# One order for all operations of an attention + gMLP kernel, from an offline search, with the eight PSUM banks given out per use

## The chip, the cores and the metric

The kernel runs on one core of one Trainium2 chip. The metric is device time in microseconds (us) of that core, the median of several executions. Before the change it was 281.91 us (three runs, 281.49 to 283.92). All medians below are of fast runs alone.

The runs of this study were made on several chips of the same kind, and the chips do not give the same time for the same program: the kernel before takes 282 to 283 us on some (283 on chip 11 of the record) and 316 to 321 us on others (chips 0 and 15). Kernels are therefore compared only with runs of the kernel before on the same chip in the same call. Where I set two chips beside each other, the text says so.

## The reference

Four batches, eight heads, 768 tokens, head dimension 64, and block-sparse attention in blocks of 32: each query block sees its neighbours, the first and the last block (the "global" ones) and three sampled blocks. The first and the last query block see all keys. A gated MLP with spatial mixing follows.

```python
mask = np.abs(blk_i - blk_j) <= 1
mask = mask | (blk_i == 0) | (blk_j == 0) | (blk_i == 23) | (blk_j == 23)
for qb in range(24):
    for kb in sampled_blocks[qb]:
        mask[qb*32:(qb+1)*32, kb*32:(kb+1)*32] = True
attn = softmax(np.where(mask, q @ k.T / sqrt(64), -1e9)) ; x = (attn @ v) as [B, 768, 512]
h = gelu(x @ w_in)                    # 512 -> 1024
u, v = h[..., :512], h[..., 512:]
v_n = layer_norm(v) * g_ln
v_s = einsum('ts,bsd->btd', w_sg, v_n) + b_sg[None, :, None]
out = x + (u * v_s) @ w_out
```

## The kernel before

The program is a list of about 1,200 named operations. Each names its engine, what it reads and writes, an estimated duration and a priority. The names recur below: `qkW qkG qkR qkQ` are score matmuls (window, global, random, and the two full query blocks), `ex*` the exponentials on ACT, `pvG pvW pvR pvQ` the products with v, `rec nrm` the normalization on DVE; `TRk TRq` transpose keys and queries and `ek eq` evict them; `xT xE` transpose and evict the attention output; `mV mU gV gU` are the first MLP matmul and its gelu, `mS g1 g2` spatial mixing and gate, `mO res` the output matmul and the residual. `ga` gathers v blocks from a scratch tensor in DRAM, `sc` writes that tensor, `vg va vs` read regular parts of it, and `kp kr` copy sampled key blocks in SBUF. A number after the name is the batch, then the tile of 128 tokens (`pvR3.0`).

A greedy list scheduler orders the operations while the kernel is built, and takes PSUM from three fixed pools:

```python
    Sps = ctx.enter_context(nc.psum_tensor("Sps", [P, 2048], F32))   # scores: two pairs of banks
    Ops = ctx.enter_context(nc.psum_tensor("Ops", [P, 1024], F32))   # PV output: one pair
    Mps = ctx.enter_context(nc.psum_tensor("Mps", [P, 1024], F32))   # all else: two banks
    pl.pool("S", 2); pl.pool("O", 1); pl.pool("M", 2)
    ...
    def schedule(self):
        ...
            for e in engs:
                cands = []
                for o in ready[e]:
                    t, s = avail(o)          # when inputs and a PSUM place are there
                    ...
                    cands.append((max(t, free[e]) + ..., o.prio, o.idx, o, s, pen))
                tmin = min(c[0] for c in cands)
                c = min((c for c in cands if c[0] <= tmin + 0.03), key=lambda c: (c[1], c[2]))
```

`emit` turns the dependences into semaphore waits and writes out, for each engine, its own list in order. Two more things matter. SyncE reads 21 block numbers into registers in one operation, ahead of the v scratch write; and some starts are held back by hand (`aft`), such as the v load of batch 1 behind the gather of block 12:

```python
    def regs_sp(e):
        for j in range(3):
            load_regs(e, "SP", j, SPSET)                              # seven blocks
        return e.dma_start(scr[1][768:800, :], scr[0][768:800, :])
    op("SP", "regsS", regs_sp, r=["IDX", ("scz", 0)], w=["regS", ("scz", 1)], ...)
    ...
    if b == 0 and i == HOLD1: hold[1] = [o]                           # ldv1 waits for this gather
```

The gate uses one buffer `gt`; `xE` of every batch runs on ACT. All matmuls but the transposes go through one helper, so their line is always L326 (L303 after): read such groups by their tiles.

The softmax here doesn't subtract the row's maximum and nothing guards it: scores larger than these inputs give would overflow.

## Time and profile before

```profile
span 314.7 us, 8868 instructions
PE 234.8 (75%) x3717; PEld 171.5 (55%) x3717; DVE 163.7 (52%) x468; ACT 149.1 (47%) x222; POOL 104.8 (33%) x204
PE   1543047597737479787699999787799997999994
PEclk9999999969795758779799999899599999999999
```

By stretches (busy time with instruction counts for the five engines, then granted clock, DMA share, GB/s):

```profile
0.00:40.00 40.00, 13.44 (x277) 10.35 (x277) 15.67 (x79) 19.19 (x26) 13.24 (x39) 1.00 0.78 252
40.00:160.00 120.00, 83.19 (x1533) 63.77 (x1532) 48.95 (x140) 55.40 (x80) 55.20 (x92) 0.82 0.72 156
160.00:300.00 140.00, 128.78 (x1871) 92.05 (x1871) 90.27 (x236) 74.52 (x116) 36.40 (x75) 0.95 0.31 78
```

TensorE is idle 27 of the first 40 us, 37 of the next 120 and 11 of the next 140. Note the span: 314.7 us, where the timed median is 281.91.

```profile
PE Sps L326 <- ACT PW L721: 4.1, 4, 2.9
PE Mps L504 <- ACT QT L512: 3.2, 4, 0.9
PE Sps L326 <- ACT PW L668: 3.0, 2, 2.7
PE Ops L326 <- issue: 2.1, 2, 1.3
```
A wait of PV for the normalization of the one output pair is in the table too, further down: 0.6 us.

```profile
80.77 0.82 ACT QT L512
...
81.63 0.54 PE Mps L504 x12
...
82.20 0.82 ACT QT L512
```

```profile
39.70 0.61 PE L326 MATMUL Sps<-QT,KR 64*128 64x32 bf16 x32 [10.32 <-POOL KR L600]
40.24 0.62 PE L326 MATMUL Ops<-VG,PG 128*128 128x130 bf16 x4
```

### The profile page before, as it was taken

Reading aid. Unit: us, or ns where it says so; the run is one execution under the profiler, and the core shown is the slowest. Engines: PE = TensorE matmul, PEld = TensorE weight load, DVE = VectorE, ACT = ScalarE, POOL = GpSimd, SP = SyncE. Lnnn points to the kernel's source line nnn. Section 1 sums busy time; section 2 is a strip of 40 time slices with the busy share of each in tenths; the row PEclk is TensorE's granted clock in tenths of the full one; section 3 lists DMA queues with packets and bytes.
Section 4 is the critical chain, followed back from the end, with each engine's and each line's share of the span. In section 5 each row is a group of like instructions: output and inputs, shape, how many; then the busy total and the mean of one; then the engine's idle time right before and its main releaser. Section 6 shows DMA issues by size and latency. Waiting matters only on the chain.

```text
span 314.7 us, 8868 instructions
## 1 busy us (share of the span) xinstructions
PE 234.8 (75%) x3717; PEld 171.5 (55%) x3717; DVE 163.7 (52%) x468; ACT 149.1 (47%) x222; POOL 104.8 (33%) x204
## 2 busy tenths in 40 slices
PE   1543047597737479787699999787799997999994
PEld 1432036485626357565355868565567675767642
DVE  6525013236533165425498657354477665758683
ACT  2587024356334752636212587455425874755200
POOL 1131777112183851542441222653403124102100
PEclk9999999969795758779799999899599999999999
DMA  6957863980999929331799102442711014111022
GB/s 205 374 164 288 230 162 78 173 133 40 195 275 242 308 33 214 86 92 38 206 210 261 64 6 50 133 122 60 211 68 32 4 27 120 37 69 35 0 100 100
DMA packets 34411, 41.29 MB, mean 131 GB/s; under 512 B 6548, under 2 KB 27700, under 8 KB 34372
## 3 DMA queue, kind: packets, MB, share of 16 engines
q0 software_dynamic: 14112, 17.40, 27.9%
q1 hardware_dynamic: 20260, 23.33, 24.0%
q8 instruction: 29, 0.48, 0.6%
q14 instruction: 10, 0.08, 0.1%
HBM read 39.45 MB, written 9.55 MB: 156 GB/s over the span
## 4 chain that ended last, share of the span: by engine, by line
PE 58%; DVE 14%; issue 11%; ACT 9%; POOL 3%; another core or an unknown queue 2%; DVEq 1%; POOLq 0%; ACTq 0%
PE Mps L326 28%; PE Ops L326 12%; PE Sps L326 9%; PE Mps L795 5%; PE Mps L504 4%; DVE gt L856 3%; ACT PR L700 2%; DVE xg L859 2%; DVE KT L512 2%; ACT QT L512 2%; POOL VR L579 1%; PE Mps L620 1%; DVE x_tok L780 1%; DVE x_tok L874 1%
## 5 line engine op out<-in xcount | busy, mean ns | idle before, releaser
L579 POOL DMA_INDIRECT VR<-scr,IDX x60 | 56.2, 937 | 56.7 <-PE Ops L326 29.7
L596 DVE COPY KR<-KT 128x128 bf16 x176 | 27.4, 230 | 38.7 <-PE Ops L326 20.8
L326 PE MATMUL Mps<-w_sgT,vh 128*128 128x384 bf16 x192 | 38.0, 345 | 2.7 <-DVE KT L512 1.8
L700 ACT ACTIVATE PR<-Sps 96x1024 bf16<-96x1024 f32 x20 | 20.4, 1020 | 32.9 <-PE Ops L326 21.6
L600 POOL COPY KR<-KT 128x128 bf16 x88 | 22.5, 296 | 39.1 <-PE Sps L326 27.1
L326 PE MATMUL Mps<-w_out,xg 128*128 128x512 f32 x96 | 28.6, 429 | 2.8 <-DVE xg L859 1.6
L326 PE MATMUL Mps<-xg,w_in 128*128 128x384 f32 x128 | 28.3, 375 | 2.5 <-ACT QT L512 2.0
L856 DVE SCALAR_TENSOR_TENSOR gt<-Mps,gcol,bsg 128x384 f32<-128x384 f32 x32 | 19.8, 618 | 17.8 <-PE Mps L326 15.6
L326 PE MATMUL Mps<-w_in,xg 128*128 128x512 f32 x96 | 27.6, 434 | 1.5 <-ACT xg L798 0.7
L326 PE MATMUL Sps<-QT,KR 64*128 64x32 bf16 x704 | 13.6, 178 | 19.2 <-POOL KR L600 9.7
L798 ACT ACTIVATE xg<-Mps 128x512 fp32r<-128x512 f32 x24 | 14.3, 596 | 28.3 <-PE Mps L795 21.0
L326 PEld LDWEIGHTS Mps<-xg,w_in 128*128 128x128 f32 x128 | 23.3, 205 | 6.9 <-ACT QT L512 2.3
L326 PEld LDWEIGHTS Mps<-w_sgT,vh 128*128 128x128 bf16 x192 | 17.6, 101 | 16.9 <-DVE KT L512 2.2
L814 ACT ACTIVATE vg<-Mps 128x512 f32<-128x512 f32 x24 | 14.0, 598 | 26.8 <-PE Mps L326 25.2
L326 PE MATMUL Sps<-QT,KT 64*128 64x64 bf16 x544 | 16.9, 209 | 12.7 <-issue 3.8
L821 POOL TENSOR_TENSOR lnt<-lnmv,lnc 128x2 f32<-128x2 f32 x12 | 3.0, 248 | 69.7 <-DVE lnmv L817 69.7
L512 DVE COPY KT<-Mps 128x768 bf16<-128x768 bf16 x16 | 15.1, 954 | 20.3 <-PE Mps L504 17.2
L326 PE MATMUL Ops<-VA,PW 128*64 128x65 bf16 x384 | 21.7, 206 | 3.9 <-issue 3.7
L326 PEld LDWEIGHTS Sps<-QT,KR 64*128 64x128 bf16 x704 | 10.9, 96 | 23.3 <-POOL KR L600 9.8
L326 PEld LDWEIGHTS Mps<-w_in,xg 128*128 128x128 f32 x96 | 18.0, 204 | 8.6 <-DVE x_tok L874 2.0
L326 PEld LDWEIGHTS Mps<-w_out,xg 128*128 128x128 f32 x96 | 16.9, 193 | 9.6 <-DVE xg L859 2.5
L326 PEld LDWEIGHTS Sps<-QT,KT 64*128 64x128 bf16 x544 | 12.1, 105 | 17.9 <-issue 5.5
(91 smaller groups left out, 414.0 us busy)
## 6 DMA issues: line engine op xcount, KB each, us to landing
out_dram<-x_tok SPq DMA_DIRECT2D x20, 256.0 KB, 2.1
scr<-vj SPq DMA_DIRECT2D x4, 780.0 KB, 5.0
VR<-scr SPq DMA_DIRECT2D x84, 32.5 KB, 3.3
VS<-scr SPq DMA_DIRECT2D x4, 650.0 KB
vn<-in_v_dram POOLq DMA_DIRECT2D x3, 768.0 KB, 9.1
kn<-in_k_dram POOLq DMA_DIRECT2D x3, 768.0 KB
qn<-in_q_dram POOLq DMA_DIRECT2D x3, 768.0 KB, 13.9
VA<-scr SPq DMA_DIRECT2D x4, 520.0 KB
```

Of the source, the lines that this page charges most:

```text
L326: return pe.matmul(o, l, r, start=start, stop=True, skip_group_check=True)
L504: ins = pe.transpose(Mbf[64 * hp:64 * hp + 64, c:c + P], n_[:, 2 * pp + hp, j, :], ident[:, :])
L512: return x.activation(o_, i_, ACT.Copy) if nm == "q" else x.tensor_copy(o_, i_)
L579: return g.indirect_dma_start(out=VR[0:96, rg, :, :].rearrange("p h e -> p (h e)"), out_offset=None, in_=scr[bp][:, :], in_offset=bass.Ind ...
L596: ins = x.tensor_copy(KR[:, :, rg, 32 * j:32 * j + 32], KT[:, :, bass.ds(vals["DVE", j, i], 32)])
L600: op("POOL", f"kp{b}.{i}", lambda x, i=i, rg=rg: x.tensor_copy(KR[:, :, rg, 64:96], KT[:, :, bass.ds(vals["POOL", 2, i], 32)]), r=kk + [(" ...
L700: return a.activation(PR[pr_][0:96, :], Sps[0:96, uR.slot * 1024:uR.slot * 1024 + 1024], ACT.Exp, scale=SCALE)
L795: ins = pe.transpose(Mps[:, cc:cc + P], x_tok[bp][:, tau, kt * P:kt * P + P], ident_f[:, :])
L798: op("ACT", f"xE{b}.{tau}", lambda a: a.activation(xg[c][:, :, tc * P:tc * P + P], Mps[:, u.slot * 512:u.slot * 512 + 512].rearrange("p (a ...
L814: op("ACT", f"gV{b}.{tau}", lambda a: a.activation(vg[vr][:, :], Mps[:, u.slot * 512:u.slot * 512 + 512], ACT.Gelu_apprx_tanh), r=[("vp", ...
L856: op("DVE", f"g1{b}.{c}{dt}", lambda x: x.scalar_tensor_tensor(gt[gr][:, :], Mps[:, u.slot * 512:u.slot * 512 + 384], gcol[:, dt:dt + 1], ...
L859: op("DVE", f"g2{b}.{c}{dt}", lambda x: x.tensor_tensor(xg[2 + c][:, dt, :], gt[gr][:, :], uT[c][:, dt, :], ALU.mult), r=[("gt", gr), ("uT ...
```

## The change

The intent: replace the greedy order by one found by a long offline search over a model of the schedule, and free the search from the PSUM pools. The whole order, with a bank for each use of PSUM, is now a string of 1,228 operations; the kernel only checks it and turns it into waits. No arithmetic is removed.

```diff
-SEMLAT = 0.07
+XE = ("DVE", "ACT", "ACT", "ACT")
...
-    def schedule(self):
-        ...                                    # the list scheduler, and the pools
+    def arrange(self, seq, bank):
+        ...
+        held = [None] * 8
+        for o in seq:
+            assert all(d.pos < o.pos for d in o.deps), o.name
+            u = o.alloc
+            if u is None: continue
+            u.slot = bank[o.name]
+            for i in range(u.banks):
+                h = held[u.slot + i]
+                if h is not None:
+                    o.deps = o.deps + [x for x in h.readers if x not in o.deps]
+                held[u.slot + i] = u
+        self.order = {e: [o for o in seq if o.eng == e] for e in ("PE", "ACT", "DVE", "POOL", "SP")}
...
+SEQ = """
+krz bias0 ones lnc zero ident0 ident1 ldq0.3 sbi ldk0.0 csq0.3 TRq0.3:3 ldv0.0 csv0.0 bias1 ix0 ldk0.1 ...
+ldq0.1 regsD1 csq0.1 TRq0.1:0 ldv1 regsP0 regsP1 regsS15 ldq0.0 csq0.0 eq0.1 regsS3 regsP2 regsS6 sc0 ...
+...                                            # 1,228 operations; ":3" is the (first) PSUM bank
...
-    gt = [sb(f"gt{i}", [P, 384], F32) for i in range(1)]
+    gt = [sb(f"gt{i}", [P, 384], F32) for i in range(2)]
-    Sps, Ops, Mps and their pools
+    PS = ctx.enter_context(nc.psum_tensor("PS", [P, 4096], F32))
-    def regs_sp(e): ...                        # 21 register loads and a DMA in one operation
+    for i in SPSET:                            # seven operations, and the DMA apart
+        op("SP", f"regsS{i}", rs_, r=["IDX"], w=[("regS", i)], ...)
-        op("ACT", f"xE{b}.{tau}", ...)
+        op(XE[b], f"xE{b}.{tau}", ...)
```

Scores and PV outputs take two neighbouring banks, all else one. The holds `aft` are ignored, so the v load of batch 1 (`ldv1`) is issued as early as its place on POOL allows.

## The prediction

> **What bounds the kernel now.** By the busy table TensorE works 234.8 of 314.7 us (75%); DVE 52%, ACT 47%, POOL 33%. By stretches TensorE is busy 13.4 of the first 40 us, 83.2 of 120 us in 40-160 (69%), 128.8 of 140 us in 160-300 (92%), 9.4 of the last 15. So the start is bound by transfers, batches 0/1 by waits, batches 2/3 nearly TensorE-bound, a tail paced by DVE. In the chain of waits TensorE has 58%, DVE 14%, issue 11%. The profiled span is 33 us over the timed median of 281.91, with a granted clock of 0.59 to 0.82 over 60-140 us. Batches 2 and 3 repeat with a 63.5 us period, so I put most of these 33 us in batches 0/1 and don't count them as gain.
>
> **What changes.** No arithmetic goes. Instruction counts and bytes stay; ACT table loads stay at about ten (1.28 us each). Six 0.6 us evictions move from ACT to VectorE.
>
> 1. Start. SyncE reads 21 registers from 13.7 to 23.7 us, and only then issues the v scratch write (24.4; landed about 30.1); TensorE idles 9.7 us until 38.6, since key copies stand behind six gathers on POOL. The change puts three of the seven register groups ahead of that write, loads v earlier, and puts key copies before gathers. I expect the write at about 20, landing at 26. Against that: batch 1's v load now has no wait ahead of it on POOL, so it issues at about 2 us, when the DMA share is already 0.96 to 1.07 (6-15 us). [...] Net: first PV matmul at 35-38 instead of 39.1; gain 2-4 us.
> 2. Batches 0/1. One output pair and two M banks become any of eight, so PV need not wait for the 0.21+0.69 us normalization, and key/query transposes (idle 0.9 us between, 88-97 us) overlap their evictions. Timed gain estimated 6-8 us.
> 3. Batches 2/3: idle is 8%, some 11 us in 140; two gt buffers and finer interleaving recover about half: 5 us.
> 4. Tail: g1/g2 pairs alternate with TensorE through one gt (0.63+0.57 us, eight times; 295-308 us). Gain 2-3 us.
>
> **On the critical path:** about 17 us of 282. [...]
>
> **Prediction:** 265 us (6% faster), 8 in 10 between 252 and 277. Faster by over 2%: 0.84; within 2%: 0.12; slower: 0.04.
>
> **What would show it.** Busy times per engine within 3% except DVE +4, ACT -4 us (clock aside); TensorE idle in 40-160 down from 37 us to under 25; idle in the batch-2/3 stretch under 7 us; scratch write issued before 22 us; first PV matmul by 38; batch-1 v load issued at about 2 us, first score matmul after 22; tail (first batch-3 gate matmul to end) near 18 instead of 21 us.
>
> **What would make it wrong.** A fixed order can't adapt: if real DMA landings or POOL times differ from the model, one late gather stalls every engine behind it and the gain of batches 0/1 goes. If the timed run already has little idle there, only start and tail count: 275. [...]

The sum came to about 17 us: 2 to 4 at the start, 6 to 8 in batches 0/1, 5 in batches 2/3, 2 to 3 in the tail.

## More of the kernel before

Below, a "fast chip" is one on which the kernel before takes 282 to 283 us, a "slow chip" one on which it takes 316 to 321.

The prediction had one profile of this kernel. Its lines, first of the page: span, busy time of each engine (share of span, instructions), TensorE's busy tenths in 40 slices of the span, and the clock that TensorE was granted, in tenths.

```profile
0.00:45.50 45.50, 15.90 (x373) 12.28 (x373) 17.67 (x90) 22.07 (x31) 16.06 (x45) 1.00 0.80 242
45.50:170.30 124.80, 101.94 (x1730) 77.25 (x1730) 68.85 (x186) 67.52 (x101) 56.76 (x95) 0.90 0.80 170
170.30:246.70 76.40, 72.70 (x1480) 54.16 (x1478) 52.93 (x151) 50.12 (x76) 28.01 (x58) 0.98 0.31 87
246.70:281.70 35.00, 29.12 (x136) 18.92 (x136) 22.71 (x43) 9.29 (x16) 2.68 (x6) 1.00 0.20 68
```

(The clock of 1.00 in the first row is not borne out by the durations of the matmuls there; the fourth call takes this up.) In the stage of batches 0 and 1 (second row) TensorE is still idle 22.9 of 124.8 us and gets 0.90 of its clock; in the next stage it is idle 3.7 of 76.4.

At the start, from the timelines of SyncE's queue and of TensorE: the scratch write is issued at 23.08 us, the reads of the global v rows at 31.29, and TensorE waits 10.32 us for key copies before its first PV matmul at 40.24.

```profile
23.08 0.56 SPq L531 DMA_DIRECT2D scr<-vj  x1
...
31.29 2.55 SPq L541 DMA_DIRECT2D VG<-scr  x4
```

The chain of waits shows the first two lines at work (start, length, what). The first piece: ACT loads a table, then runs an exponential, and only then the score matmuls get the place in `Sps` that it frees. The second: a query transpose fills one of the two `Mps` banks and must wait for an eviction each time.

```profile
69.13 1.28 ACT L721
...
70.42 1.03 ACT PW L721
...
71.50 0.61 PE Sps L326 x16
```

The run that was profiled took 316.53 us itself. So the profile is no distorted copy of the timed runs but an honest record of a slower run. The prediction had to guess where the 33 us lay.

That can be settled by a control made later: the same kernel, unchanged, profiled on a chip where it takes 283 us (experiment c0_before). All comparisons with the kernel after use this profile. (It is of another call than the result's, but of the same speed: the kernel before takes 283.12 us there and 282.3 in the result.) Its page lines, and its stretches, cut at landmarks of the work (first normalized tile of batch 0, first of batch 2, last of batch 3):

```profile
span 281.7 us, 8868 instructions
PE 219.7 (78%) x3717; PEld 162.6 (58%) x3717; DVE 162.2 (58%) x468; ACT 149.0 (53%) x222; POOL 103.5 (37%) x204
PEclk9999999999795759997999999999799999999999
```

## The result, and the profile after

| | before | after |
|---|---|---|
| time, median of 4 fast runs each | 282.3 us (281.49 to 283.92) | 250.3 us (249.55 to 251.99) |
| ratio, 95% interval | | 0.887 (0.880 to 0.893) |
| span of the profile used here | 281.7 us | 247.7 us |
| mean granted clock in it | 0.952 | 0.977 |

Ratios are the mean time of one kernel's fast runs over that of the other's of the same rounds, so not quite the ratio of the medians quoted. Executions over 1.5% slower than the fastest of the same kernel are left out of the means. The change brought 32 us where 17 were predicted, and 250.3 lies just below the range that should have held it (252 to 277).

The page and the stretches of the kernel after, cut at the same landmarks:

```profile
span 247.7 us, 8892 instructions
PE 205.8 (83%) x3717; PEld 158.6 (64%) x3717; DVE 159.9 (65%) x474; ACT 142.3 (57%) x216; POOL 110.2 (44%) x204
PEclk9999999989999979999999997999999999999999
```

```profile
0.00:40.60 40.60, 14.14 (x300) 11.25 (x301) 18.00 (x79) 18.66 (x26) 18.93 (x47) 1.00 1.01 276
40.60:147.30 106.70, 97.52 (x1899) 75.82 (x1897) 73.91 (x215) 69.15 (x104) 57.43 (x96) 0.97 0.89 190
147.30:216.20 68.90, 67.35 (x1380) 50.87 (x1378) 45.91 (x140) 46.05 (x70) 31.14 (x55) 0.98 0.37 103
216.20:247.70 31.50, 26.80 (x145) 20.64 (x143) 22.05 (x44) 8.45 (x17) 2.67 (x6) 0.98 0.23 84
```

Side by side, in us (lengths from the two tables of stretches; idle is length less TensorE busy):

| stage | before | after | gain | predicted gain | TensorE idle before, after |
|---|---|---|---|---|---|
| start, to first tile of batch 0 | 45.5 | 40.6 | 4.9 | 2 to 4 | 29.6, 26.5 |
| batches 0/1, to first tile of batch 2 | 124.8 | 106.7 | **18.1** | **6 to 8** | 22.9, 9.2 |
| batches 2/3, to last tile of batch 3 | 76.4 | 68.9 | 7.5 | 5 | 3.7, 1.6 |
| tail | 35.0 | 31.5 | 3.5 | 2 to 3 | 5.9, 4.7 |
| sum | 281.7 | 247.7 | 34.0 | 17 | 62.0, 41.9 |

Three of the four terms came out within some 2.5 us of what was said; one is more than twice too small. Inside it, the first normalized tile of batch 1 comes at 111.2 us before and at 91.3 after: 15.0 of the 18.1 us lie between the first tiles of batches 0 and 1. The stages do not hold quite the same work, since the new order moves matmuls between them (counts in brackets: 1730 in batches 0/1 before, 1899 after, 100 fewer in batches 2/3), so the split into stages is good to a few us only. That is also why batches 2/3 could gain 7.5 us with only 3.7 us of idle time: part of their work is now done earlier.

Of the 34.0 us, TensorE's idle time gave 20.1 and its busy time 13.9 (219.7 to 205.8), with the same 3717 matmuls. Weighing the busy time of each 1-us window of the two profiles with what its recorded clock lacks of full speed, I estimate 11.5 us lost to the clock before and 4.9 after: 6.6 of the 13.9. (The sum leaves out the start, where the recorded clock fails; TensorE is busy there for 15.9 and 14.1 us, so little of the difference can hide in it.) So busy time was no fixed quantity of work here: it shrank by 6% without any work taken away. The other 7.3 us I have not taken apart.

The waits of the batch-0/1 stage after the change answer to the four lines shown of before:

```profile
PE PS L303 <- issue: 6.4, 4, 3.4
PE PS L303 <- DVE QT L493: 0.9, 1, 0.9
PE PS L303 <- DMA VG<-scr: 0.6, 1, 0.6
```

No wait for an exponential to free a score place, none for an eviction to free a transpose bank is left among them. What remains is mostly "issue", time for which the profile shows no cause. Its largest piece, 3.39 us at 45 us, lies inside one group of 32 score matmuls, after the third of them; `emit` puts a group's semaphore waits before its first matmul only.

At the start (queue of SyncE, then TensorE):

```profile
19.60 0.36 SPq L510 DMA_DIRECT2D scr<-vj  x1
...
28.60 1.40 SPq L520 DMA_DIRECT2D VG<-scr  x2
```

```profile
26.56 1.03 PE L303 MATMUL PS<-QT,KT 64*128 64x64 bf16 x32 [2.80 <-DVE QT L493]
...
37.81 0.62 PE L303 MATMUL PS<-VG,PG 128*128 128x130 bf16 x4 [5.54 <-DMA VG<-scr]
```

The scratch write is issued 3.5 us earlier, the first PV matmul comes 2.4 us earlier, and in exchange the first score matmul slipped from 19.79 (timeline of c0_before) to 26.56, as predicted (after 22).

### The profile page after: what moved, and what is told of

Same layout as the page of the kernel before. It is cut to its first block, busy times and chain, and to the rows that moved or that the text cites. A ratio compares the mean times of both kernels' runs of the same rounds, so it can differ in the third digit from the quotient of the medians.

```text
span 247.7 us, 8892 instructions
## 1 busy us (share of the span) xinstructions
PE 205.8 (83%) x3717; PEld 158.6 (64%) x3717; DVE 159.9 (65%) x474; ACT 142.3 (57%) x216; POOL 110.2 (44%) x204
## 4 chain that ended last, share of the span: by engine, by line
PE 67%; DMA 17%; issue 5%; SPq 4%; POOL 2%; DVE 2%; ACT 1%
PE PS L303 58%; DMA uT<-in_v_dram 5%; PE PS L774 5%; DMA x_tok<-in_moe_w_sg_dram 5%; PE PS L483 4%; DMA VG<-scr 3%; DMA VR<-scr,IDX 3%; SPq L445 1%; POOL VR L558 1%; ACT vj L460 1%; SPq L520 1%; SPq L390 1%; DMA scr<-VG 1%; POOL KR L579 1%; PE PS L599 1%
## 5 line engine op out<-in xcount | busy, mean ns | idle before, releaser
L303 PE MATMUL PS<-w_sgT,vh 128*128 128x384 bf16 x192 | 35.2, 332 | 0.0
L679 ACT ACTIVATE PR<-PS 96x1024 bf16<-96x1024 f32 x20 | 20.3, 1021 | 12.4 <-PE PS L303 12.4
L303 PE MATMUL PS<-xg,w_in 128*128 128x384 f32 x128 | 27.4, 348 | 0.0
L303 PE MATMUL PS<-w_in,xg 128*128 128x512 f32 x96 | 26.9, 408 | 0.0
L303 PE MATMUL PS<-w_out,xg 128*128 128x512 f32 x96 | 26.8, 409 | 0.0
L838 DVE SCALAR_TENSOR_TENSOR gt<-PS,gcol,bsg 128x384 f32<-128x384 f32 x32 | 19.6, 616 | 9.5 <-PE PS L303 8.9
L303 PEld LDWEIGHTS PS<-w_sgT,vh 128*128 128x128 bf16 x192 | 17.6, 99 | 11.5 <-issue 0.7
L303 PEld LDWEIGHTS PS<-xg,w_in 128*128 128x128 f32 x128 | 22.2, 188 | 2.0 <-ACT xg L780 0.4
L796 ACT ACTIVATE vg<-PS 128x512 f32<-128x512 f32 x24 | 14.1, 601 | 11.5 <-PE PS L303 11.0
L659 ACT ACTIVATE PG<-PS 128x512 bf16<-128x512 f32 x24 | 14.0, 600 | 10.1 <-PE PS L303 10.1
L303 PEld LDWEIGHTS PS<-QT,KT 64*128 64x128 bf16 x544 | 11.5, 104 | 12.9 <-issue 5.0
L303 PEld LDWEIGHTS PS<-w_out,xg 128*128 128x128 f32 x96 | 17.0, 188 | 3.4 <-DVE xg L841 0.2
L303 PE MATMUL PS<-VA,PW 128*64 128x65 bf16 x384 | 18.4, 203 | 0.0
```

Of the source, the lines that this page charges most:

```text
L303: return pe.matmul(o, l, r, start=start, stop=True, skip_group_check=True)
L659: op("ACT", f"exG{b}.{tau}", aft=ga, fn=lambda a: a.activation(PG[pg_][:, :], PS[:, uG.slot * 512:uG.slot * 512 + 512], ACT.Exp, scale=SCALE),
L679: return a.activation(PR[pr_][0:96, :], PS[0:96, uR.slot * 512:uR.slot * 512 + 1024], ACT.Exp, scale=SCALE)
L796: op("ACT", f"gV{b}.{tau}", lambda a: a.activation(vg[vr][:, :], PS[:, u.slot * 512:u.slot * 512 + 512], ACT.Gelu_apprx_tanh), r=[("vp", b ...
L838: op("DVE", f"g1{b}.{c}{dt}", lambda x: x.scalar_tensor_tensor(gt[gr][:, :], PS[:, u.slot * 512:u.slot * 512 + 384], gcol[:, dt:dt + 1], b ...
```

## The experiments

Theory A: with the same engines at the same speed, the old order left about 23 us of idle time in batches 0/1 even on a fast chip; the new order and its banks fill most of it, and some of the clock dips go with it. I had taken that idle time for a fault of the first profile. Rival B: the eight banks alone do it, in any order. Rival C: the start is what counts, and shifts everything behind it. Rival D: it is the clock.

### First call: what the first profile was worth, and order against banks (before: 283.12 us)

**c0_before**: the kernel before, unchanged.

> The kernel before, unchanged, as a control with a clean profile. Expected 282 us (281 to 284). The first profile of it spanned 314.7 us at a granted clock of 0.91, 33 us over the timed runs. Theory A (the 33 us are a clock and trace matter of that one execution): this profile spans about 280 at a clock above 0.95, and TensorE idles 25 to 30 us less between 40 us and the end of batch 1. Rival B (timed runs are like the first profile in their idle share): the profile again spans over 300.

Measured: 283.18 us, ratio 1.0005 (0.996 to 1.005), span 281.7. TensorE idle 24.0 of 100 us between 40 and 140. Span and clock are as Theory A had them; the idle time is not: from 40 us to the last tile of batch 1 it falls from 34.6 to 22.4 us, 12 us less and not 25 to 30. The lines are shown above. By landmarks, the first profile's surplus of 33 us lay as follows: 2.6 us before the first tile of batch 0 (48.1 against 45.5), 19.0 in batches 0/1 (143.8 against 124.8), 11.5 in batches 2/3 (87.9 against 76.4), none in the tail. So "most" of it was in batches 0/1, as the prediction had it, but taking it away still leaves 22.9 us of idle time there, and of the 23.2 us that the first profile lost to the clock, 11.5 are lost on the fast chip as well.

**b_banks8**: the old order, eight banks given out by least recent use, one `gt`, `xE` on ACT. It tests rival B by itself.

```diff
-    pl.schedule()
+    SEQ = the order that schedule() gives for the kernel before, written out
+    bank  = the least recently used of eight, for each use of PSUM
-XE = ("DVE", "ACT", "ACT", "ACT")
+XE = ("ACT", "ACT", "ACT", "ACT")
```

> The order of before on all engines, but each PSUM use takes the least recently used of eight banks; one gt buffer, all xT evictions on ACT as before. Order theory: 277 to 283 us. Bank theory: 268 us or less.

Measured: 273.86 us, ratio 0.971 (0.964 to 0.978). Free banks in the old order are worth 3%, a quarter of the gain. Between the two theories. Of its profile, the stage of batches 0 and 1:

```profile
45.20:164.40 119.20, 99.47 (x1729) 76.78 (x1730) 70.23 (x187) 67.17 (x101) 55.82 (x94) 0.90 0.83 177
```

This stage takes 124.8 us in c0_before, on the same chip, and 119.2 here: 5.6 us by the banks alone.

**b_greedy8**: the old scheduler run again, with eight banks to choose from instead of pools.

```diff
-                pl = self.pools[o.alloc.pool]
-                for s in range(len(pl["held"])):
+                for s in (range(8) if n == 1 else (0, 2, 4, 6)):
+                    us = [held8[s + i] for i in range(n)]
+                    ...                        # with at most four banks for scores, four for outputs
```

> The old list scheduler run again with eight banks (scores and single-bank uses at most four each, outputs at most four), so the old rule makes a new order with the new freedom. Order theory (the search itself matters): 270 to 280 us. Bank theory (any scheduler with eight banks gets it): 262 us or less.

Measured: 269.04 us, ratio 0.951 (0.945 to 0.956), just better than the range of the order theory. A greedy order made for eight banks is worth 5%. The remaining 6 points belong to the searched order with its own banks; the second `gt` buffer, which this variant lacks, is in them too. The stage of batches 0 and 1 takes 113.3 us, 11.5 less than in c0_before:

```profile
44.90:158.20 113.30, 93.96 (x1776) 75.05 (x1772) 66.87 (x187) 64.68 (x100) 58.27 (x96) 0.89 0.89 187
```

**a_psum_old**: the new order on the old pools. Where a use found no free place in its pool, the operation had to move back: 75 of 343 TensorE operations change place, by at most 7; on the other engines 162 of 885, by at most 10.

```diff
-TRk0.0:1 ... TRk0.1:6 ... qkW0.0:4 ... pvG0.0:6
+TRk0.0:6 ... TRk0.1:7 ... qkW0.0:0 ... pvG0.0:4     # scores 0-1 or 2-3, output 4-5, all else 6 or 7
```

> The new order, but PSUM given out as before (two score pairs, one output pair, two single banks); operations are only put back as far as a missing bank demands (75 of 343 TensorE steps change place, by 7 places at most). Order theory (the gain is the order on the engines): 252 to 258 us, most of the 32 us stays. Bank theory (the gain is that PSUM may be given to any use): 268 us or more, over half of the gain goes.

Measured: 347.09 us in its one fast run, slower than any theory allowed: 23% over the kernel before. The other three (356.21 to 359.77) count as slow, since they lie over 1.5% above it, so there is no interval. The profile is of one of the slow three (mean clock 0.837, against 0.876 in the fast run), so it shows what kind of waits there are and not how much each costs the fast run. Its clock row, and what TensorE waits for after 45 us:

```profile
PEclk9999999786799967658579998995555999558999
```

```profile
PE PS L304 <- ACT QT L492: 7.4, 9, 0.9
PE PS L304 <- DVE x_tok L760: 6.4, 6, 2.0
PE PS L304 <- ACT uT L824: 5.2, 9, 0.6
```

TensorE waits for the readers of PSUM: for the evictions of query transposes, for the normalization of the one output pair (`x_tok`), for the gelus of MLP outputs. So the searched order is not a better order in itself; it is one that needs free banks. (An order searched for the old pools was not tried, and the repair here is a simple one.) Order and banks are not two gains that add: banks without the order give 3%, the order without the banks costs 23%, both give 11%.

### Second call: where in the run (another chip; before: 321.05 us)

**hyb_a_then_b**: the new order up to the first normalized tile of batch 1 (431 operations), then the old one, with eight banks. **hyb_b_then_a**: the reverse (456 operations). They tell a local gain from a shift that everything later inherits. In the first, the banks before the seam are the searched ones and 172 of the 200 after it were chosen anew; in the second, 247 of all 283 were.

```diff
-SEQ = new
+SEQ = new[:431] + [o for o in old if o not in new[:431]]       # hyb_a_then_b
+SEQ = old[:456] + [o for o in new if o not in old[:456]]       # hyb_b_then_a
```

> The new order up to the first normalized tile of batch 1 (431 operations), then all the rest in the order of before, with eight banks. By the landmarks of the two profiles this tile comes at 111.2 us before and 91.3 us after, so stage-local theory: 282 less about 20, 258 to 266 us. Rival (the gain needs the whole order, because the new order hands less work on at the seam): 270 us or more.

> The order of before up to the first normalized tile of batch 1 (456 operations), then the rest in the new order, eight banks. Stage-local theory: 282 less about 14, 264 to 272 us, plus what eight banks alone give the first part (0 to 5 us less). Rival: 275 us or more.

Measured: 286.5 us, ratio 0.893 (0.886 to 0.901), and 294.9, ratio 0.920 (0.910 to 0.930). The expectations had been written for a fast chip, so compare ratios. The gains are 10.7% and 8.0%. They sum to 18.7%, and the whole change is worth 18.8% on a chip of this speed (c1_after, next call), but that agreement is in part luck: both variants hold some of what eight banks give to the old order, and neither has the searched banks throughout. The landmarks say more. The times until the first normalized tile of batch 1, and from there to the end (us; all at the slow chips' speed, though not all on one chip):

| | to this tile | rest |
|---|---|---|
| kernel before (first profile) | 124.9 | 189.8 |
| hyb_a_then_b | 93.0 | 193.5 |
| hyb_b_then_a | 120.0 | 173.1 |
| kernel after (c1_after) | 92.9 | 166.6 |

With the new order first, the early gain is all there and the rest is about as long as before (3.7 us longer). With the new order last, the rest gains 16.7 us although the start is the old one; 4.9 of the gain lie before the seam, where only the banks are new. So the gain is made where the order differs and is not handed on. For the whole change the tile comes 32.0 us earlier and the rest gains 23.2, so 58% is made before it; the profiles of the fast chips say the same (4.9 + 15.0 of 34.0 us, 59%). Rival C in its strong form is out.

**a_lru8**: the new order, but the banks chosen anew by a rule close to least recent use; 248 of 283 choices differ.

```diff
-TRq0.3:3 ... TRk0.0:1 ... qkW0.0:4 ...     # banks from the search
+TRq0.3:b ... TRk0.0:b ... qkW0.0:b ...     # b chosen anew; 248 of 283 differ
```

> The new order unchanged on every engine, but the bank of 248 of the 283 PSUM uses chosen anew (roughly least recently used). If only order and freedom count: 250 to 253 us. Rival (the search tuned the banks to the order, so that a bank is free when its use comes up): 257 us or more.

Measured: 280.32 us, ratio 0.875 (0.865 to 0.884). At first sight this is the ratio of the change itself, 0.887. That was wrong: the 0.887 is from a chip where the kernel before takes 282 us, this one from a chip where it takes 321. The next call corrects it.

**b_start**: the kernel before, with three of SyncE's seven register groups and the DMA that stood with them moved behind the scratch write and its reads.

```diff
 SyncE:
-regsS3 regsS6 regsS9 regsS12 regsS15 regsS18 regsS21 scz1 sc0 vg0 va0 vs0
+regsS3 regsS6 regsS9 regsS12 sc0 vg0 va0 vs0 regsS15 regsS18 regsS21 scz1
```

> The kernel before with its own order and PSUM pools; on SyncE alone three of seven register groups and one small copy move behind the v scratch write and reads. I expect the scratch write to issue at 20 to 21 us instead of 24.4 and the whole to take 2 to 4 us less: 278 to 281 us. If start transfers are limited by the DMA engines and not by that issue: no change, 282 to 284 us.

Measured: 315.6 us, ratio 0.981 (0.971 to 0.992). The scratch write went out at 19.77 us (24.43 in the first profile, which is the one of a slow chip to compare with). So the point that the prediction made of it holds, and it is worth between 0.8 and 2.9% by the interval. (This variant, like b_banks8, uses the new program's way of turning a given order into waits; no run tests that by itself, so its share is within this figure.)

### Third call: the change on a slow chip, and the start (before: 318.34 us)

**c1_after**: the kernel after, unchanged.

> The changed kernel again, as the control of this call: chips differ (the kernel before took 282 us on one chip and 321 on another). Expected ratio to before 0.87 to 0.90 on a chip where before takes 282. If the chip is like the slow one (before near 320, with idle that the trace puts down to no engine): ratio 0.82 to 0.90.

Measured: 258.92 us, ratio 0.812 (0.807 to 0.817). On this chip the kernel before takes 36 us more than on the fast one, the kernel after only 8 to 9.

**a_lru8_again**: the same kernel as a_lru8, now beside c1_after.

```diff
 (as a_lru8)
```

> The new order with the banks chosen anew, repeated beside its control, since the first time it ran on another chip. If only order and freedom count: within 1% of the changed kernel of this call. If banks are tuned to the order: over 4% slower, with TensorE waiting for evictions for 15 to 30 us in all.

Measured: 279.75 us, ratio 0.881 (0.875 to 0.886). Against c1_after the other banks cost 8.0% by the medians (279.75 / 258.92) and 8.5% by the ratios. TensorE's idle time rises from 47.3 us (span 259.5) to 61.4 us (span 275.8). Its largest waits after 45 us:

```profile
PE PS L303 <- issue: 7.2, 12, 1.8
PE PS L303 <- DVE gt L838: 3.1, 3, 2.0
PE PS L774 <- DVE x_tok L759: 2.8, 2, 1.7
```

Beside "issue", which c1_after has as well (7.8 us), these are waits for the reader of a bank: the order is the same, but a matmul now stands behind a normalization or a gate that has not yet read the bank it was given. So the bank numbers are part of the searched result.

**a_ldv_late**: `ldv1` behind the gather of block 10, with the operations that need it (`vc1`, `sc1`) later.

```diff
-... TRq0.1:0 ldv1 regsP0 ...      ... ga0.10 pvG0.0:6 ...
+... TRq0.1:0 regsP0 ...           ... ga0.10 ldv1 pvG0.0:6 ...
```

> The changed kernel, with batch 1's v load moved on POOL from about 2 us to behind the tenth gather (about 33 us), and its copy and scratch write moved back with it. If the early load costs what I predicted [...]: first score matmul at 21 to 23 instead of 26.6 us, scratch write issued near 17 instead of 19.6. If that delay is on the critical path, the whole takes 2 to 4 us less; if the first PV matmul is held by the queue of v reads on SyncE: within 1 us of the changed kernel.

Measured: 256.75 us, ratio 0.804 (0.796 to 0.812), about 1% or 2 us under c1_after; the intervals overlap (0.807 to 0.817 there), so in the whole time this is no difference that the runs can tell. The scratch write comes at 15.79 us, the first score matmul at 22.77, the first PV matmul at 35.11. In c1_after, on the same chip, these are 18.56, 25.65 and 37.52. So a load issued on POOL's queue at 2 us, which nothing needs before batch 1, delayed what hangs on the loads of SyncE's queue by 2.4 to 2.9 us.

**a_start_all**: in addition, the zero rows of the scratch are written before the v rows, the four global v reads and two more v reads stand before the first gather on SyncE, one register group is read later, and `w_in` stands behind five gathers on POOL.

```diff
-regsS15 regsS3 regsS6 sc0 regsS12 ... w_in ... scz0 ga0.3 vg0.0 va0.0 vg0.2 vs0 vg0.3 vg0.1
+scz0 regsS15 regsS3 regsS6 sc0 vg0.0 vg0.2 ... w_in (after five gathers) vg0.3 vg0.1 va0.0 vs0 ga0.3 regsS12
```

> As the late v load, and besides: the zero-row write before the v scratch write, the four global v reads and the two v reads before the first gather on SyncE, w_in behind the first five gathers on POOL. If the start is held by the order of these transfers: first PV matmul at 28 to 32 instead of 37.8 us, and 4 to 9 us less in all (near 243 where the changed kernel takes 250). If by the DMA engines' rate or the gathers: 36 us or later, and no gain.

Measured: 253.05 us, ratio 0.795 (0.790 to 0.800): 2.0% under c1_after by the ratios, 2.3% by the medians, and the intervals do not meet. It beats both kernels. The first PV matmul runs at 28.06 us without a wait; some of that is given back at 40 us, where a gather is late (TensorE's timeline):

```profile
28.06 0.62 PE L303 MATMUL PS<-VG,PG 128*128 128x130 bf16 x4
...
40.38 0.63 PE L303 MATMUL PS<-VR,PR 96*32 96x65 bf16 x32 [4.10 <-DMA VR<-scr,IDX]
```

The first PV matmul comes 9.5 us earlier than in c1_after, the first normalized tile 7.4 us (35.0 against 42.4), and the time is 5.9 us shorter: with the start mended, a wait for a gather (4.10 us) is the largest one there. So a search by a model can leave a simple thing on the table, here the order of a handful of DMA issues.

### Fourth call: the clock and the rest (before: 318.61 us)

**c2_after**: the kernel after once more, as the control of this call.

> Control of this call: the changed kernel. 250 us beside 282 of before on the usual chip, 258 to 262 beside 318 on the slow one.

Measured: 258.25 us, ratio 0.812 (0.809 to 0.816), mean clock 0.989.

**a_stall**: the kernel after with two added gaps in TensorE's dense stretch. Each is a chain of two tiny DMAs that a TensorE step waits for. It tests rival D: if gaps cost clock, these must cost more than their length.

```diff
+    for n, key, held in ((1, ("sW", 3, 4), "pvR3.0"), (3, ("vp", 3, 1), "xT3.5")):
+        dly(n, [key])                                # 512 bytes DRAM to SBUF
+        stalls[held] = dly(n + 1, [("dly", n)])      # and again; then "held" may start
```

> The changed kernel with two idle gaps added to TensorE on purpose, at about 197 and 220 us where it has none: there one group of matmuls waits for a chain of two tiny transfers after the group before it (about 5 us each). Clock theory (idle lowers the granted clock, so a gap costs more than its length): after each gap the granted clock is below 0.7 for 3 to 4 us, busy time of TensorE grows by 2 to 4 us, and the whole by 12 to 15 us. Rival (idle costs only itself, and clock dips come by chance): no new dips, busy time within 1 us, 8 to 10 us in all.

Measured: 266.91 us, ratio 0.835 (0.831 to 0.840), 8.66 us over the control. The gaps came out smaller than I had sized them, 2.58 and 2.63 us. The first of them in TensorE's timeline, and windows of 1 us around it (columns as above; the clock is the third number from the end):

```profile
211.88 0.48 PE L304 MATMUL PS<-VR,PR 96*32 96x65 bf16 x32 [2.58 <-DMA stl<-in_moe_b_sg_dram]
```

```profile
210.00:211.00 1.00, 0.00 (x0) 0.00 (x0) 0.00 (x1) 0.00 (x0) 0.00 (x0) 1.00 0.00 1
...
213.00:214.00 1.00, 1.00 (x3) 0.81 (x4) 0.73 (x2) 0.69 (x1) 0.60 (x1) 0.50 0.28 59
214.00:215.00 1.00, 1.00 (x6) 0.48 (x5) 0.38 (x4) 0.00 (x0) 0.00 (x0) 0.50 0.66 184
...
216.00:217.00 1.00, 1.00 (x56) 0.87 (x49) 0.69 (x4) 1.00 (x2) 0.55 (x2) 1.00 0.58 152
```

During the gap the column still reads 1.00; when work comes back it runs at 0.50 for about 3.4 us, and then at 1.00. The same follows the second gap; the control has no such dip there. Gaps of 5.2 us and 3.3 us of busy time lost to the clock (1.6 to 1.7 each) make 8.5, against 8.66 measured by the medians, 2.9% or some 7.4 us by the ratios. (The runs of this variant spread over 3 us, so the fit is no closer than that.) Each of these two waits in a dense stretch cost its own length and some 1.65 us more.

Rival D is thereby put in its place: on these two waits the clock put a surcharge of some 3.3 us in all. But not every wait pays it, and not every dip follows one long wait. In c1_after a wait of 1.50 us at 158 us is followed by a dip and one of 1.82 us at 92 us is not; in c0_before the dip at 85 us follows three waits of 0.91 us each. What decides is not shown by these runs. By the sum above, the recorded clock stands for 6.6 of the 34.0 us.

One caution on the column. In c0_before it reads 1.00 through the first 45 us, but the matmuls there are not at full rate. The first profile, whose column also reads 1.00 at the start, shows it: a matmul of the first PV group takes 315 ns there (median, at 39 us), 315 in a recorded dip (115 to 119 us, 0.50) and 222 in the dense stretch (150 to 195 us); transposes of keys take 314, and 219 when dense. In b_banks8, where the column reads 0.50 at that place (in each window of 4 us from 28 to 48 us), the same group is just as long as in c0_before (0.62 us at 40.24, above):

```profile
38.74 0.62 PE L303 MATMUL PS<-VG,PG 128*128 128x130 bf16 x4
```

So the matmuls of the start were as slow as those that the column puts at 0.50, and the column of c0_before missed it.

**a_xe_act**: `xE` of batch 0 back on ACT.

```diff
-XE = ("DVE", "ACT", "ACT", "ACT")
+XE = ("ACT", "ACT", "ACT", "ACT")
```

> The changed kernel with the six xT evictions of batch 0 on ACT again, at the same places of the order. Expected within 1% of the control (0 to 2 us more): in that stage neither engine is over 75% busy. If the move to VectorE mattered: over 3 us more.

Measured: 259.08 us, ratio 0.814 (0.811 to 0.818), 0.3% over the control: no difference that these runs can tell. This part of the change shows no gain by itself.

**a_best**: a_start_all with `w_in` behind eight gathers and the k and v loads of batch 1 later still, to free the late gather.

```diff
-ga0.1 ga0.7 ga0.5 w_in ...      ga0.11 ldv1 pvG0.2:2 ldk1 ...
+ga0.1 ga0.7 ga0.5 ...           ga0.11 w_in ... ga0.14 ldk1 ... ga0.16 ldv1
```

> The early start of before (late v load, zero rows and global v reads first), with w_in behind eight gathers and batch 1's v and k loads behind the gathers that tile 2 of batch 0 waits for. There the first start variant waited 4.1 us. Expected 6 to 10 us less than the control; if that wait only moves to another transfer, 5 to 7 us less, as the first variant.

Measured: 254.83 us, ratio 0.806 (0.801 to 0.811), 0.8% under its control by the ratios, where a_start_all was 2.0% under its own. The late gather is earlier: the second normalized tile comes at 39.8 us (43.2 in a_start_all). But by the fifth tile this is lost (61.0 against 60.4). A miss: a_start_all stays the best kernel tried.

## Why the prediction was wrong

The direction was right, and so were the mechanisms that were named: transposes no longer wait for evictions, PV is freed, the start gains. One term of the sum priced only half of the change, and the clock had no term in it.

1. **The step that failed: "Batches 0/1 ... Timed gain estimated 6-8 us".** It was 18.1 us. The term names freed banks only ("one output pair and two M banks become any of eight"), and for banks alone it was near: in b_banks8, old order with free banks, this stage gains 5.6 us. A greedy order made for the eight banks gains 11.5 there, the searched order with its banks 18.1. So 12.5 us came with operations in another order and the banks fitted to it, which the term did not have. The waits show the same: for the control's largest one in this stage, score matmuls waiting for an exponential to free a place in `Sps` (4.1 + 3.0 us), the prediction had no term; the wait of PV for the normalization, which it named, was 0.6 us.

   A second ground for the small figure stood before: "I put most of these 33 us in batches 0/1 and don't count them as gain". The control shows that 19.0 of the 33 us did lie there, but as 10.1 us of idle time and 8.8 us of longer TensorE busy time. So 22.9 us of idle time remain in this stage on the fast chip (33.0 in the first profile), of which the change removed 13.7. A further 4.4 us came from a shorter TensorE busy time (101.9 to 97.5), which the sum did not have at all. Between 40 and 160 us the idle time was 36.8 us in the first profile, 24.8 on the fast chip, and 10.7 after the change ("under 25" was said).
2. **The clock: not in the sum.** The mean clock rose from 0.952 to 0.977. The two added gaps show that a wait can bring a dip; that the filled waits account for the whole rise is not shown. Counting it would have added 6.6 us, by the sum above.
3. **"Busy times per engine within 3% ... (clock aside)": wrong.** TensorE fell by 6.3%, about half of it clock. POOL rose by 6.4% (103.5 to 110.2), ACT fell by 6.7 us instead of 4, DVE fell by 2.3 instead of rising by 4.
4. **Start, "gain 2-4 us": 4.9.** Scratch write at 19.60 (said: before 22), first PV matmul at 37.81 (by 38), `ldv1` at 2.1 (about 2), first score matmul at 26.56 (after 22). All four signs are there. The early load was counted rightly as a cost, and a_ldv_late, which loads later, has its first score matmul 2.9 us earlier.
5. **Batches 2/3, "5 us": 7.5**, partly work moved to the stage before. Idle there 1.6 us (under 7 was said).
6. **Tail, "Gain 2-3 us": 3.5** by the last tile. From the first gate matmul of batch 3 to the end the profile after has 19.0 us (near 18 was said).
7. **"A fixed order can't adapt"**, the risk I named, was not what happened. On a slow chip the fixed order lost 8 to 9 us where the greedy one, which is just as fixed once it is built, lost 36.

What settles it: order and banks belong together (0.971 for banks alone, 0.951 for a greedy order on eight banks, 0.887 for the searched order with its banks, 1.23, by one fast run, for that order without them, and 8% lost for the same order with other bank numbers), and each half of the new order gains where it stands (32.0 us before the first tile of batch 1, kept by the one hybrid; 16.7 of 23.2 us after it, by the other).

What stays open: 7.3 us of TensorE's busy time that went without a change of the recorded clock, the share of the second `gt` buffer, which no run takes back alone, and what makes some chips slower. In the first profile the chain of waits has stalls of about 3.5 us put down to "another core or an unknown queue" (3.54 us at 260.11). It also has more "issue" gaps inside groups of matmuls (about 20 us in the first profile, 4 in the control). No run here tells why, nor why the kernel after suffers less from it.

## What to carry to other kernels

When the profiled span and the timed median differ, look first at the time of the profiled run itself: if it was slow too, you have a true profile of slower conditions, and should get one under those you are timed in before discounting anything. Idle time on the limiting engine, in a stage that it should bound, is what a better order can win (13.7 of 22.9 us in batches 0/1 here), and freeing buffers in the old order wins only a part of it (5.6 of 18.1 us here). A wait in a dense stretch can cost more than its length, here some 1.65 us for each of two. An order and the buffers it was found with are one result: transplant both or neither, and look afterwards at the first 40 us by hand.
